# A's scores and softmax split and placed among Newton's steps, q and k loads planned nine steps earlier, W' chunks spread over the batch

## The chip, the cores and the metric

The kernel runs on one core of a Trainium2 chip. The metric is the device time of one execution in microseconds. The core has a matmul engine (TensorE; PE in the profile, with its weight loads as PEld), VectorE (DVE), ScalarE (ACT), GpSimd (POOL), and SyncE (SP), whose queue here issues all data transfers. Each engine works off its own instructions in a fixed order; an instruction that waits holds up everything behind it on that engine.

## What is computed

Three blocks in a row: attention over 32 landmarks for 8 batches of 8 heads, an MLP with an ELU, and a maxout MLP.

```python
q_lm = q.reshape(B, H, m, S // m, D).mean(axis=3)      # B=8, H=8, S=576, D=64, m=32
k_lm = k.reshape(B, H, m, S // m, D).mean(axis=3)
A, Bm, C = sm(q, k_lm), sm(q_lm, k_lm), sm(q_lm, k)    # softmax of scaled scores
Z = Bm.T / (norm1(Bm) * norminf(Bm) + 1e-06)
for _ in range(6):
    Z = 2 * Z - Z @ Bm @ Z
x = heads_to_columns(A @ Z @ C @ v)                    # 4608 x 512
h = x @ w_in                                           # 512 -> 2048
g = where(h > 0, h, exp(min(h, 0)) - 1)
x = g @ w_out                                          # 2048 -> 512
out = maximum(x @ w1, x @ w2, x @ w3) @ w_out2
```

## The kernel before

Fp32 is reached with three matmuls of split operands (high times high, low times high, high times low). The first phase covers attention and the first MLP, the second the maxout MLP; the change touches the first.

**Steps.** The main loop at the end of the kernel function runs 256 steps, 32 for each batch (`NSL`): two halves of 288 tokens times 16 blocks of 128 hidden columns. A step t issues `h_mm` (6 matmuls into `ph`, read from the softmax rows `ah`, `al` and the folded weights W', tile `wp`), then whatever the list `plan[t]` holds, then `h_post` (the end of the ELU on VectorE, tile `eh`, and its split into `gt`), then `x_mm` of step t-3 (12 matmuls into four accumulators `x`). ScalarE does two activations of `eh` and a cast per step. `ph` has two buffers: the `h_mm` of a step needs the `h_post` of the step two earlier.

**Attention.** While batch b-1 goes through its 32 steps, `att_steps(b)` computes what batch b needs: the sums over 18 tokens of q and k (`sums`), C's scores and exponentials (`score_c`), their transposes (`exp_t`), C times v (`cv`), the 32x32 softmax and its norms (`soft_b` to `norm_b`), `bbt`, six Newton steps (`newton`, n0 to n5), A's scores (`score_a`, two halves of 288 tokens, each read from the q tile and transposed on VectorE), A's softmax for two groups of heads (`soft_a1` subtracts the maximum and exponentiates, `soft_a2` sums, `soft_a3` scales, transposes into `af` and splits into `ah` and `al`), and `m_step`, which ends the Newton chain. Then `w_step(b, n)` makes W' chunk n of four: 16 matmuls into the two `banks`, two ScalarE casts, two VectorE subtractions. Chunk n serves hidden blocks 4n to 4n+3; the first `h_mm` of batch b needs chunk 0. All these matmuls pass through the same two PSUM `banks` (in the first stage other ones).

**Loads.** `load_qk` brings a batch's q and k for one group of heads (576 KB each) into tiles of two buffers per tag: one batch's two groups fill both, so the loads of batch b+1 reuse the tiles that A's scores of batch b still read. `Narrowing` converts the second phase's weights twice in each of batches 1 to 6 (batches count from 0): a load of 1 MB into the tile that also holds v (one buffer, free once `cv` of the batch has read v), a burst of four ScalarE activations (L114, L117), two VectorE shifts (L123), two GpSimd additions (L127), a store.

**Order.** The tables `STEP_SLOTS` (batches 2 to 7) and `SECOND_SLOTS` (batch 1) give each attention step the number of a main-loop step; but the final order on every engine is set by the framework's scheduler, which places each instruction by its own estimate of when its operands are there, with the program's order as priority. What then stands where is read from the finished program.

Of the kernel before, what the change touches and what calls it, by code (L numbers as in the profile page):

```python
# [19 lines left out]
def landmark_attention_mlp_maxout_kernel(  # L20
# [336 lines left out]
    def score_a(b):  # L357
        xs_ = [
            att.tile([P, 2 * NB2, M], F32, tag="s", name="x", bufs=3) for _ in range(2)
        ]  # L360
        for half in range(2):
            pas = att_pair(b, "pa")
            heads(
                pas,
                HF,
                lambda j: state["ks", b, j // 2][:, j % 2],
                lambda j: state["q", b, j // 2][:, j % 2, half * HF : (half + 1) * HF],
            )
# [702 lines left out]
    def att_steps(b):  # L1071
# [20 lines left out]
        first += [("a", lambda: score_a(b)), ("m", lambda: m_step(b))]  # L1092
# [17 lines left out]
    def load_att(b):  # L1110
# [72 lines left out]
    for _ in range(NF):  # L1183
# [208 lines left out]
```

## Time and profile before

| | us |
|---|---|
| median of 3 runs (1420.45 to 1422.23) | 1421.42 |
| the profiled execution, its own time | 1420.76 |
| span of its trace, first to last instruction | 1418.6 |
| TensorE busy in the span | 1322.1 (93%) |
| VectorE, GpSimd, ScalarE busy | 868.7, 692.6, 686.6 |

TensorE is the busiest engine. The first phase takes up to some 850 us of the span, in which a batch's 32 steps take 99 to 100 us once all is running. The profile shows for each wait who ended it, and, in slices, the clock that TensorE was granted as a share of full speed (1.00 is 2.4 GHz, 0.50 is 1.2 GHz).

### The profile page before, as it was taken

The numbers are of one execution on the slowest core, as the hardware profiler recorded it, in microseconds if no ns is written. First come the engines' busy times: TensorE is split into PE (matmuls) and PEld (weight loads), VectorE is DVE, ScalarE is ACT, GpSimd is POOL, SyncE is SP. The second block draws the span as 40 slices with busy tenths as digits, with TensorE's granted clock in tenths as the row PEclk, the third lists the DMA queues.
The fourth block names the chain that finished last, engine by engine and source line by source line (L and its number), as shares of the span: only waits on it lengthen the run. The fifth ranks groups of instructions, "written<-read, shape, count | busy, mean of one in ns | idle before, by whom it ended". The sixth has DMA issues, their size and how long they took to land.

```text
span 1418.6 us, 28407 instructions
## 1 busy us (share of the span) xinstructions
PE 1322.1 (93%) x11144; PEld 1236.2 (87%) x11144; DVE 868.7 (61%) x1597; ACT 686.6 (48%) x1554; POOL 692.6 (49%) x677
## 2 busy tenths in 40 slices
PE   2498999899899999898999899899999999999998
PEld 1288899699699698797897899899999999998998
DVE  5866643643644635536445757866776677687773
ACT  4676566455565655664665573322222222335551
POOL 2783334234333333342343566665666666675543
PEclk8589999899999999999999999999999999999999
DMA  9623304203214023033032113212221222148972
GB/s 367 219 73 101 101 18 140 85 26 115 84 41 159 25 88 120 18 113 112 1 107 77 45 33 105 96 53 108 82 83 74 87 83 109 75 141 299 302 253 76
DMA packets 91591, 152.31 MB, mean 107 GB/s; under 512 B 5312, under 2 KB 49472, under 8 KB 91456
## 3 DMA queue, kind: packets, MB, share of 16 engines
q1 hardware_dynamic: 91456, 150.49, 31.0%
q8 instruction: 87, 1.43, 0.4%
q14 instruction: 48, 0.39, 0.1%
HBM read 99.35 MB, written 51.12 MB: 106 GB/s over the span
## 4 chain that ended last, share of the span: by engine, by line
PE 72%; DVE 11%; DMA 5%; issue 4%; ACT 4%; POOL 3%; SPq 0%; DVEq 0%; POOLq 0%; ACTq 0%
PE x L660 23%; PE p L935 23%; PE ph L629 13%; PE p L1044 8%; PE banks L226 5%; POOL u L816 1%; DMA words<-in_moe_w_in_dram 1%; DVE wp L606 1%; DMA hf<-hs 1%; DVE tt L744 1%; DMA qT<-in_q_dram 1%; DMA words<-in_moe_w_dram 1%; DMA kT<-in_k_dram 1%; ACT words L117 1%; DVE af L403 1%
## 5 line engine op out<-in xcount | busy, mean ns | idle before, releaser
L660 PE MATMUL x<-gt,wo 128*128 128x288 f32 x3072 | 467.7, 299 | 4.2 <-ACT xo L686 2.9
L660 PEld LDWEIGHTS x<-gt,wo 128*128 128x128 f32 x3072 | 427.8, 190 | 17.4 <-issue 9.2
L935 PE MATMUL p<-xo,w 128*128 128x256 f32 x3402 | 412.6, 284 | 4.7 <-ACT xo L777 1.7
L935 PEld LDWEIGHTS p<-xo,w 128*128 128x128 f32 x3402 | 410.2, 191 | 7.1 <-ACT xo L777 3.3
L98 POOL TENSOR_TENSOR gt<-eh,gt 128x288 fp32r<-128x288 f32 x243 | 199.6, 825 | 369.2 <-ACT gt L96 339.9
L629 PE MATMUL ph<-ah,wp 128*128 128x288 f32 x1024 | 262.1, 311 | 22.6 <-ACT ah L96 9.8
L629 PEld LDWEIGHTS ph<-ah,wp 128*128 128x128 f32 x1024 | 183.8, 195 | 63.7 <-DVE eh L639 22.1
L639 DVE SCALAR_TENSOR_TENSOR eh<-eh,ph 128x288 f32<-128x288 f32 x256 | 114.9, 452 | 194.0 <-ACT eh L634 173.5
L816 POOL TENSOR_TENSOR u<-s,v 128x512 f32<-128x512 f32 x99 | 137.2, 1386 | 138.1 <-DVE v L814 138.1
L96 ACT CAST gt<-eh 128x288 fp32r<-128x288 f32 x256 | 110.3, 432 | 105.8 <-DVE eh L639 105.6
L629 PE MATMUL ph<-al,wp 128*128 128x288 f32 x512 | 156.1, 306 | 2.6 <-POOL al L98 2.5
L633 ACT ACTIVATE eh<-ph 128x288 f32<-128x288 f32 x256 | 103.8, 410 | 107.7 <-PE ph L629 95.5
L805 ACT COPY s<-p 128x512 f32<-128x512 f32 x99 | 58.0, 586 | 182.5 <-PE p L935 152.1
L1044 PE MATMUL p<-wo,ho 128*128 128x256 f32 x1134 | 136.6, 283 | 5.1 <-ACT ho L1032 3.8
L1044 PEld LDWEIGHTS p<-wo,ho 128*128 128x128 f32 x1134 | 136.0, 190 | 5.7 <-ACT ho L1032 4.2
L634 ACT ACTIVATE eh<-eh 128x288 f32<-128x288 f32 x256 | 112.7, 445 | 5.8
L629 PEld LDWEIGHTS ph<-al,wp 128*128 128x128 f32 x512 | 99.7, 195 | 6.1 <-POOL al L98 5.6
L829 DVE TENSOR_TENSOR t<-p,u 128x512 f32<-128x512 f32 x81 | 55.7, 687 | 65.9 <-POOL u L816 63.0
L942 DVE TENSOR_TENSOR t<-t 128x1024 f32<-128x1024 f32 x54 | 71.5, 1324 | 8.8 <-POOL t L819 3.2
L1034 DVE TENSOR_TENSOR ho<-hf,ho 128x768 fp32r<-128x768 f32 x54 | 66.3, 1254 | 16.3 <-ACT ho L1032 15.8
L127 POOL TENSOR_TENSOR wf<-wf,words 128x512 uint32<-128x512 uint32 x40 | 53.2, 1333 | 40.5 <-ACT words L117 28.8
L1032 ACT CAST ho<-hf 128x768 fp32r<-128x768 f32 x63 | 51.6, 837 | 43.2 <-PE p L1044 23.6
(162 smaller groups left out, 1438.2 us busy)
## 6 DMA issues: line engine op xcount, KB each, us to landing
hf<-hs SPq DMA_DIRECT2D x63, 384.0 KB, 5.2
hs<-t SPq DMA_DIRECT2D x27, 512.0 KB, 2.6
xs<-xo SPq DMA_DIRECT2D x36, 288.0 KB, 2.9
hs<-s SPq DMA_DIRECT2D x27, 384.0 KB, 2.9
qT<-in_q_dram SPq DMA_DIRECT2D x16, 576.0 KB, 5.8
kT<-in_k_dram SPq DMA_DIRECT2D x16, 576.0 KB, 7.0
words<-in_moe_w_dram SPq DMA_DIRECT2D x9, 1024.0 KB, 6.2
xf<-xs SPq DMA_DIRECT2D x9, 1024.0 KB, 5.0
```

The lines of the kernel that those rows point to most:

```text
L96: nc.scalar.copy(hi, src)
L98: eng.tensor_tensor(out=lo, in0=src, in1=hi.bitcast(F32), op=ALU.subtract)
L226: ins = fn(*args, **kw)
L629: nc.tensor.matmul(ph[:, :HF], a, c, start=(g == 0 and j == 0), stop=(g == 1 and j == 2))
L633: nc.scalar.activation(e, ph[:, :HF], AF.Relu, scale=-1.0)
L634: nc.scalar.activation(e, e, AF.Exp, scale=-1.0)
L639: nc.vector.scalar_tensor_tensor(out=e, in0=e, scalar=1.0, in1=ph[:, :HF], op0=ALU.subtract, op1=ALU.max)
L660: nc.tensor.matmul(xacc[ec][:, :HF], a, gt[:, c], start=(first and j == 0), stop=(last and j == 2),)
L816: nc.gpsimd.tensor_tensor(out=u57, in0=s57, in1=v.unsqueeze(1).to_broadcast([P, 2, 256]), op=ALU.add)
L935: nc.tensor.matmul(dst, l, r, start=(c == 0 and j == 0), stop=(c == 1 and j == 2))
L942: nc.vector.tensor_tensor(out=t, in0=t, in1=cur, op=ALU.max)
L1044: nc.tensor.matmul(dst, l, r, start=(c == 0 and n == 0), stop=(c == NP - 1 and n == 2))
```

## The change

`score_a` becomes two steps, `ah0` and `ah1`, one per half of the tokens, planned at steps 10 and 12 (before: one step at 18), between Newton's steps 9 to 14 (before 12 to 17). The softmax pieces of the two groups alternate and each group has its own small tile `t18`. `sums` of batch b move to the last steps of the batch ahead (-6 to -3, before 0 to 3) and the loads of q and k to -9; v stays at 0. The four W' chunks of the next batch are planned at steps 21, 25, 29 and 33, two after the last reader of their place (before 26, 28, 30 and 32). Nothing is computed otherwise; the number of matmuls, transfers and bytes is the same.

```diff
-    def score_a(b):
-        xs_ = [
-            att.tile([P, 2 * NB2, M], F32, tag="s", name="x", bufs=3) for _ in range(2)
-        ]
-        for half in range(2):
-            pas = att_pair(b, "pa")
-            heads(
...
+    def score_a(b, half):
+        if not half:
             for g in range(2):
...
+        pas = att_pair(b, "pa")
+        heads(
...
         for g in range(2):
-            state["x", b, g] = xs_[g]
+            x = state["x", b, g][:, half * NB2 : (half + 1) * NB2]
+            nc.vector.transpose(out=x.rearrange("p a m -> p (a m)"), in_=pas[g][:, :HF])
...
-        t = att.tile([P, 2 * NB2], F32, tag="t18", name="t18")
+        t = att.tile([P, 2 * NB2], F32, tag=f"t18{g}", name="t18")
...
-        first += [("a", lambda: score_a(b)), ("m", lambda: m_step(b))]
+        first += [("ah0", lambda: score_a(b, 0)), ("ah1", lambda: score_a(b, 1)), ("m", lambda: m_step(b))]
...
     STEP_SLOTS = dict(
...
-        bbt=11, n0=12, n1=13, n2=14, n3=15, n4=16, n5=17, a=18, m=19, a10=19, a20=20, a30=20,
-        a11=21, a21=22, a31=23,
+        bbt=8, n0=9, n1=10, n2=11, n3=12, n4=13, n5=14, ah0=10, ah1=12, m=15, a10=12, a11=13,
+        a20=14, a21=15, a30=17, a31=18,
...
+    W_SLOTS = [-11, -7, -3, 1]
 
     def load_att(b):
         for g in range(2):
             load_qk(b, g, "q")
             load_qk(b, g, "k")
-        load_v(b)
...
         if b > 1:
-            at(t0, load_att, b)
+            at(t0 - 9, load_att, b)
+            at(t0, load_v, b)
...
         for n in range(NCH):
-            at(t0 + NSL + 2 * n - 6, w_step, b, n)
+            at(t0 + NSL + W_SLOTS[n], w_step, b, n)
```

What the scheduler makes of it, at four places. Rows give line, operation, output<-inputs and shape; most code lines stand three lower in the changed program (`h_mm` L629 becomes L626, `x_mm` L660 becomes L657).

**The end of the batch ahead of batch 4, TensorE.** `rr` and `rd` are a Newton step's operands, `bbd` is read by `m_step`, `w_in_sb` by a W' chunk. Before, from `m_step` on:

```order
L226 MATMUL banks<-bbd,rr_94 64x128 x2
L629 MATMUL ph<-ah,wp 128x288
L660 MATMUL x_5084<-gt,wo 128x288 x3
L660 MATMUL x_5085<-gt,wo 128x288 x3
L660 MATMUL x_5086<-gt,wo 128x288 x3
L660 MATMUL x_5087<-gt,wo 128x288 x3
L660 MATMUL x_5084<-gt,wo 128x288 x3
L660 MATMUL x_5085<-gt,wo 128x288 x3
L660 MATMUL x_5086<-gt,wo 128x288 x3
L226 MATMUL banks<-w_in_sb,mt 32x512 x8
L660 MATMUL x_5087<-gt,wo 128x288 x3
```

After, around `m_step` and chunk 0:

```order
L657 MATMUL x_5116<-gt,wo 128x288
L657 MATMUL x_5117<-gt,wo 128x288
L226 MATMUL banks<-bbd,rr_94 64x128 x2
L226 MATMUL banks<-w_in_sb,mt 32x512 x8
L626 MATMUL ph<-ah,wp 128x288
L626 MATMUL ph<-al,wp 128x288
L626 MATMUL ph<-ah,wp 128x288
```

and around chunks 1 and 2, four h matmuls further on:

```order
L626 MATMUL ph<-ah,wp 128x288 x2
L626 MATMUL ph<-al,wp 128x288
L226 MATMUL banks<-w_in_sb,mt 32x512 x8
L626 MATMUL ph<-ah,wp 128x288 x2
L226 MATMUL banks<-w_in_sb,mt 32x512 x8
L626 MATMUL ph<-ah,wp 128x288
L626 MATMUL ph<-al,wp 128x288
```

Before, 21 x matmuls stand between `m_step` and chunk 0, 27 more behind it, and only then the new batch's `h_mm`. After, the last Newton step stands 12 x matmuls ahead of the old batch's end, `m_step` behind the last of these, chunk 0 behind `m_step`, the new batch's `h_mm` behind chunk 0; and two h matmuls stand between chunks 1 and 2 (before: six).

**The same place, VectorE.** From the transposes of A's second half on (`t_...` are A's maxima and sums, L270 the q and k sums of the next batch). Before:

```order
L370 STREAM_TRANSPOSE x<-banks 128x288 x2
L381 TENSOR_REDUCE t_5076<-x 128x18
L383 TENSOR_TENSOR x<-x,t_5076 128x576
L270 TENSOR_REDUCE qs<-qT 128x64
L639 SCALAR_TENSOR_TENSOR eh<-eh,ph 128x288
L390 TENSOR_REDUCE t_5110<-x 128x18
L270 TENSOR_REDUCE kT<-kT 128x2x32
```

After, up to the addition of the last but one Newton step:

```order
L378 TENSOR_REDUCE t_4897<-x 128x18
L380 TENSOR_TENSOR x<-x,t_4859 128x576
L636 SCALAR_TENSOR_TENSOR eh<-eh,ph 128x288
L270 TENSOR_REDUCE qs<-qT 128x64
L380 TENSOR_TENSOR x<-x,t_4897 128x576
L270 TENSOR_REDUCE kT<-kT 128x2x32
L513 TENSOR_TENSOR rd<-banks,hm 128x256
L387 TENSOR_REDUCE t_4930<-x 128x18
L636 SCALAR_TENSOR_TENSOR eh<-eh,ph 128x288
L270 TENSOR_REDUCE qs<-qT 128x64
L387 TENSOR_REDUCE t_4964<-x 128x18
L270 TENSOR_REDUCE kT<-kT 128x2x32
```

The four sums still stand between the pieces of A's softmax; two Newton operations (this `rd` and, some rows further on, the additions L566) have come among them, and the W' subtractions (L606, now L603), four of which stood before the second `af`, have gone behind it.

**Batch 0, VectorE.** Around main-loop steps 20 to 25, while batch 1's attention runs. Before:

```order
L639 SCALAR_TENSOR_TENSOR eh<-eh,ph 128x288
L370 STREAM_TRANSPOSE x<-banks 128x288 x2
L381 TENSOR_REDUCE t_1491<-x 128x18
L639 SCALAR_TENSOR_TENSOR eh<-eh,ph 128x288
L270 TENSOR_REDUCE qs<-qT 128x64
```

After:

```order
L372 STREAM_TRANSPOSE x<-banks 128x288 x2
L603 TENSOR_TENSOR wp<-banks,wp 128x512 x2
L372 STREAM_TRANSPOSE x<-banks 128x288 x2
L378 TENSOR_REDUCE t_1390<-x 128x18
L270 TENSOR_REDUCE qs<-qT 128x64
L378 TENSOR_REDUCE t_1431<-x 128x18
L636 SCALAR_TENSOR_TENSOR eh<-eh,ph 128x288 x2
L513 TENSOR_TENSOR rd<-banks,hm 128x256
```

A's scores have moved four steps ahead there, on both sides of a W' chunk of batch 0, and the first q sum of batch 2 has come ahead of two `eh`.

**The middle of a batch, ScalarE.** The second conversion burst, before:

```order
L96 CAST gt<-eh 128x288
L114 ACTIVATE wf_5272<-words_5185 128x512
L117 ACTIVATE words_5185<-words_5185 128x512
L114 ACTIVATE wf_5275<-words_5185 128x512
L117 ACTIVATE words_5185<-words_5185 128x512
L633 ACTIVATE eh<-ph 128x288
```

and after:

```order
L630 ACTIVATE eh<-ph 128x288
L564 COPY rr_94<-banks 128x2x32
L114 ACTIVATE wf_5314<-words_5209 128x512
L117 ACTIVATE words_5209<-words_5209 128x512
L114 ACTIVATE wf_5317<-words_5209 128x512
L631 ACTIVATE eh<-eh 128x288
L117 ACTIVATE words_5209<-words_5209 128x512
```

The burst now stands three steps behind the batch's first burst (before four) and between the two activations of one step's `eh`. The first burst stands behind the two ScalarE copies of `x` into `xo` in the middle of the batch (before: ahead of them).

## Rows read from the trace of the kernel before

**Rows 1.** The page, its first line.
```profile
span 1418.6 us, 28407 instructions
```
**Rows 2.** TensorE by stretches: start:end, length, busy us, granted clock, DMA share, GB/s.
```profile
378.80:458.40 79.60, 79.53 (x710) 1.00 0.23 77
260.00:282.00 22.00, 17.79 (x131) 0.77 0.20 72
...
460.00:482.00 22.00, 18.68 (x149) 0.84 0.16 59
...
660.00:682.00 22.00, 16.98 (x140) 0.92 0.18 66
760.00:782.00 22.00, 20.14 (x177) 1.00 0.42 124
```
**Rows 3.** Chain that ended last: start, us, what; a Newton step, an h step, an x step.
```profile
445.66 0.44 PE banks L226 x4
...
446.24 0.79 PE ph L629 x6
...
450.12 1.62 PE x L660 x12
```
**Rows 4.** TensorE in time at the batch's end: start, us, instruction [idle before].
```profile
453.52 0.71 PE L226 MATMUL banks<-qT,kT 64*32 64x288 f32 x16
...
466.67 1.09 PE L226 MATMUL banks<-w_in_sb,mt 64*32 64x512 f32 x16 [0.28 <-DVE wp L606]
...
470.58 1.73 PE L226 MATMUL banks<-w_in_sb,mt 64*32 64x512 f32 x16 [1.09 <-DVE wp L606]
473.81 0.85 PE L629 MATMUL ph<-ah,wp 128*128 128x288 f32 x2 [1.51 <-ACT ah L96]
```
**Rows 5.** VectorE in time there: the second `af`.
```profile
472.52 0.78 DVE L403 STREAM_TRANSPOSE af<-x 128x576 f32<-128x576 f32 x1
```
**Rows 6.** VectorE groups from 454.3 to 473.4: count, busy us, mean ns, idle before.
```profile
L270 DVE TENSOR_REDUCE qs<-qT 128x64 f32<-128x1152 f32 x2 | 2.7, 1350 | 1.4 <-DMA qT<-in_q_dram 1.4
...
L606 DVE TENSOR_TENSOR wp<-banks,wp 128x512 fp32r<-128x512 f32 x4 | 2.6, 680 | 0.0
```
**Rows 7.** VectorE groups of the whole span: a Newton step's `rd`.
```profile
L516 DVE TENSOR_TENSOR rd<-banks,hm 128x256 f32<-128x256 f32 x35 | 14.7, 420 | 9.9 <-PE banks L226 9.6
```
**Rows 8.** Waits of the SP queue: line, waited for, us, times, longest.
```profile
SPq L252 <- PE banks L226: 83.0, 5, 16.9
```
**Rows 9.** ScalarE groups from 454.3 to 473.4: the casts of W' and `ah`.
```profile
L601 ACT CAST wp<-banks 128x512 fp32r<-128x512 f32 x5 | 2.7, 586 | 2.4 <-PE banks L226 2.3
...
L96 ACT CAST ah<-af 128x288 fp32r<-128x288 f32 x3 | 1.2, 429 | 1.3 <-DVE af L403 1.3
```
**Rows 10.** TensorE in time at batch 0's steps 20 to 26.
```profile
141.94 0.71 PE L226 MATMUL banks<-rr,rd 128*128 128x128 f32 x4 [1.10 <-DVE rr L569]
...
149.72 0.72 PE L226 MATMUL banks<-qT,kT 64*32 64x288 f32 x16
```
**Rows 11.** VectorE in time there: the first q sum.
```profile
154.63 1.35 DVE L270 TENSOR_REDUCE qs<-qT 128x64 f32<-128x1152 f32 x1 [2.22 <-DMA qT<-in_q_dram]
```
**Rows 12.** TensorE in time in the middle of batches 1 and 4.
```profile
214.27 0.90 PE L226 MATMUL banks<-v,et 128*32 128x64 f32 x40
...
512.81 0.90 PE L226 MATMUL banks<-v,et 128*32 128x64 f32 x40
...
524.40 0.67 PE L660 MATMUL x<-gt,wo 128*128 128x288 f32 x3 [1.45 <-ACT xo L686]
```
**Rows 13.** ScalarE in time there: first activations of the conversion bursts.
```profile
220.24 0.69 ACT L114 ACTIVATE wf<-words 128x512 f32<-128x512 f32 x1 [0.17 <-DMA words<-in_moe_w_dram]
...
520.44 0.67 ACT L114 ACTIVATE wf<-words 128x512 f32<-128x512 f32 x1 [2.59 <-DMA words<-in_moe_w_dram]
...
531.49 0.67 ACT L114 ACTIVATE wf<-words 128x512 f32<-128x512 f32 x1 [2.19 <-DMA words<-in_moe_w_dram]
```
**Rows 14.** VectorE in time: the `eh` behind the second burst of batch 4.
```profile
534.73 0.46 DVE L639 SCALAR_TENSOR_TENSOR eh<-eh,ph 128x288 f32<-128x288 f32 x1 [0.24 <-ACT eh L634]
```

More of the change, by code (lines that the diff above doesn't have):

```diff
@@ L355, in score_c2 @@
         state["rs", b, g] = rs
-    def score_a(b):
-        xs_ = [
-            att.tile([P, 2 * NB2, M], F32, tag="s", name="x", bufs=3) for _ in range(2)
-        ]
-        for half in range(2):
-            pas = att_pair(b, "pa")
-            heads(
[L364 to L368, printed above, removed]
+    def score_a(b, half):
+        if not half:
             for g in range(2):
-                nc.vector.transpose(
-                    out=xs_[g][:, half * NB2 : (half + 1) * NB2].rearrange("p a m -> p (a m)"),
-                    in_=pas[g][:, :HF],
-                )
+                state["x", b, g] = att.tile(
+                    [P, 2 * NB2, M], F32, tag="s", name="x", bufs=3
+                )
+        pas = att_pair(b, "pa")
+        heads(
+            pas,
+            HF,
+            lambda j: state["ks", b, j // 2][:, j % 2],
+            lambda j: state["q", b, j // 2][:, j % 2, half * HF : (half + 1) * HF],
+        )
         for g in range(2):
-            state["x", b, g] = xs_[g]
+            x = state["x", b, g][:, half * NB2 : (half + 1) * NB2]
+            nc.vector.transpose(out=x.rearrange("p a m -> p (a m)"), in_=pas[g][:, :HF])
     def soft_a1(b, g):
@@ L388, in soft_a2 @@
     def soft_a2(b, g):
-        t = att.tile([P, 2 * NB2], F32, tag="t18", name="t18")
+        t = att.tile([P, 2 * NB2], F32, tag=f"t18{g}", name="t18")
         nc.vector.tensor_reduce(out=t, in_=state["x", b, g], op=ALU.add, axis=AX.X)
@@ L1099, in landmark_attention_mlp_maxout_kernel @@
     STEP_SLOTS = dict(
-        q0=0, k0=1, q1=2, k1=3, c=5, c20=6, c21=6, e0=6, cv0=7, e1=8, b=8, b2=9, cv1=10, nb=10,
-        bbt=11, n0=12, n1=13, n2=14, n3=15, n4=16, n5=17, a=18, m=19, a10=19, a20=20, a30=20,
-        a11=21, a21=22, a31=23,
+        q0=-6, k0=-5, q1=-4, k1=-3, c=2, c20=3, c21=3, e0=3, cv0=4, e1=5, b=5, b2=6, cv1=7, nb=7,
+        bbt=8, n0=9, n1=10, n2=11, n3=12, n4=13, n5=14, ah0=10, ah1=12, m=15, a10=12, a11=13,
+        a20=14, a21=15, a30=17, a31=18,
     )
@@ L1105, in landmark_attention_mlp_maxout_kernel @@
         q0=4, k0=5, q1=6, k1=7, c=8, c20=9, c21=9, e0=9, cv0=11, e1=11, b=12, b2=12, cv1=13, nb=13,
-        bbt=13, n0=13, n1=14, n2=15, n3=16, n4=18, n5=19, a=20, m=20, a10=21, a20=23, a30=24,
-        a11=26, a21=26, a31=26,
+        bbt=13, n0=13, n1=14, n2=15, n3=16, n4=18, n5=19, ah0=16, ah1=17, m=20, a10=18, a11=19,
+        a20=20, a21=21, a30=22, a31=23,
     )
+    W_SLOTS = [-11, -7, -3, 1]
     def load_att(b):
@@ L1199, in landmark_attention_mlp_maxout_kernel @@
         "V": [lambda g=g, fn=fn: fn(0, g) for g in range(2) for fn in (score_c2, exp_t, cv)],
-        "A": [lambda: score_a(0)]
+        "A": [lambda: [score_a(0, half) for half in range(2)]]
         + [
@@ L1228, in landmark_attention_mlp_maxout_kernel @@
     load_att(1)
+    load_v(1)
     def after_gate(stp):
```

## The prediction

> **What bounds the kernel now.** I read the page first, then TensorE by stretches, then its idle times in order, then what the engines ahead of it did there. The span is 1418.6 us [rows 1]. In the 80 us between two batch ends TensorE is busy 79.53 of 79.60 us at full clock [rows 2]: there only fewer matmuls would help, and the change removes none. An h step costs 0.79 us and an x step 1.62 [rows 3]. What can be won is at the batch ends. In 22 us around each, TensorE is idle 4.2 us ahead of batch 2, 3.3 ahead of batch 4, 5.0 ahead of batch 6, 1.9 ahead of batch 7 (length less busy time) [rows 2]; batches 3 and 5 lie between 4 and 6. I call these ends 2 to 7, by the batch that follows. The granted clock of these stretches, 0.77, 0.84, 0.92 and 1.00, means 10.1, 7.0, 3.5 and 0 us at 1.2 GHz [rows 2].
>
> Why it idles: the second half of A's scores ends near 454.2 [rows 4], and VectorE works without a pause from there until the second `af` at 473.3 [rows 5], except 1.4 us in which the first q sum waits for its load [rows 6]. Two q sums (2.7 us), two k sums like them, four W' subtractions (2.6) and both groups' softmax stand in that one queue [rows 6]; `h_mm` waits for the `ah` at its end (1.51 us), and chunks 1 and 2 for the subtractions of the chunks ahead (0.28 and 1.09) [rows 4]. The plan of the change would break up this queue. What the order shows decides whether it does.
>
> **The loads.** The plan has them nine steps early, but the tile is the one that A's scores of the batch ahead read. SP already waits for TensorE at L252 in 5 batches, 83.0 us in all [rows 8], and the load goes out when A's second half has been read. That half is no earlier in the new order: five and a third x steps ahead of the batch's end before, five and two thirds after, because Newton's chain starts later and is stretched. So q lands some 4 us behind A's end (the first q sum began at 154.63, where A's second half had started at 149.72 and taken 0.72 [rows 10, 11]), and the sums stay where they were in the queue.
> The Trainium skill, DMA: Bandwidth & Descriptors, section Rules for kernel authors, says to issue a transfer early and wait for it late; its section Anatomy of one DMA says that a semaphore wait happens on the issuing sequencer before the transfer is dispatched. The 83.0 us of [rows 8] agree with the second and speak against the first helping here. By the first rule no q sum would wait, and the sum below would be some 4 us smaller, an estimate.
>
> **Ends 3 to 6.** Take A's end as 0. VectorE's list up to the second `af` is the old one (19.1 us, 454.2 to 473.3) without the four W' subtractions (-2.6) [rows 6], with one `eh` (0.46 [rows 14]), one `rd` (0.42) and two additions on half as many columns (0.6 taken) more [rows 7]; and the q sum stands some 1 us further back, so that its wait shrinks from 1.4 to about 0.4. That is 17.0. ScalarE then casts the second group's `ah` twice (0.43 each, the second partly beside the first) and only then chunk 0's high part (0.59) [rows 9], since chunk 0 is now made at the very end: `h_mm` can start near 18.5. TensorE's work up to there is 3 h steps (2.4), 5.67 x steps (9.2), two Newton steps (0.44 each [rows 3]), `m_step` (no more than one of these) and chunk 0 (1.09 [rows 4]), 14.0. So 4.5 us idle, spread over Newton's last step, which waits for an addition queued behind the sums, `m_step`, chunk 0 and `h_mm`. Then chunk 2: before, 2.8 us passed from chunk 1's end (467.76) to chunk 2 (470.58) for two casts and two subtractions [rows 4], with six h matmuls between. After, two (0.27): 2.5 us idle. Together 7.0 against 4.2 (the middle of [rows 2]): +2.8 for each of four ends, +11. The clock I take as before; the idle pieces are longer, so the upper bound has +3 each for it, and the lower bound 0 for the whole place, were VectorE's list 3 us shorter than its rows say.
>
> **End 2.** A's second half stands two x steps earlier, so the chain to chunk 0 finds cover. Two `eh` behind the sums hold up `h_mm` for some 1.9 us and chunk 2 for 2.5: 4.4, against 4.2. But this end has had 10.1 us at the lower clock, the others about 5 [rows 2]; half of the difference is -2. Bounds -5 and +1.
>
> **End 7.** No sums here. Chunk 0 directly ahead of `h_mm` costs its cast and a latency (0.9), chunk 2 again 2.5: 3.4, against 1.9. +2, bounds 0 and +4.
>
> **Batch 0.** The largest single piece. A's scores move ahead to where batch 0 makes its own last W' chunk with nothing else left for TensorE: the two transposes between cost 0.9. Behind A's second half VectorE meets the first q sum at once. Before, that sum began 4.2 us behind A's end (154.63, A ends near 150.4) [rows 10, 11], of which VectorE idled 2.2, and the last `eh` had gone through ahead of it. Now two `eh` stand behind it: 4.2 + 1.35 + 0.7 (a maximum) + 0.4 = 6.6 us until TensorE's next `h_mm` may start, with 0.7 us of work: 5.9 idle. The next two `eh` stand behind three more sums, two reductions, `rd` and an addition, near 13.5, when TensorE has run out near 11.9: 1.6. Less the 1.10 that a Newton step waited there [rows 10]: 0.9 + 5.9 + 1.6 - 1.1 = 7.3, and 2 more for the lower clock behind so long a gap. +9, bounds +4 and +12.
>
> **The middle of batches 1 to 6.** The first conversion burst starts when its load lands behind `cv`: 5.1 us behind it in batch 1 (220.24 against 215.1), 6.7 in batch 4 (520.44 against 513.7) [rows 12, 13]; four batches are like the first, two like the second. In those two the burst held up the copies of `x` for 1.45 us [rows 12]; the copies now stand ahead of it: -2.9 in all. The second burst starts 11.05 us behind the first (531.49 less 520.44) [rows 13], as its load needs the tile back, and the `eh` behind it ends 3.7 us later (535.19) [rows 13, 14]. Counted from `cv`, that is 5.1 or 6.7 + 14.75 = 19.9 or 21.5. By the new order TensorE needs that `eh` after 6 h steps (4.7), 7.33 x steps (11.9), `bbt` and two Newton steps (1.3 [rows 3]) and A's first half (0.7 [rows 4]): 18.6. Stall 1.3 or 2.9; before none, since the burst stood a step later. 4 x 1.3 + 2 x 2.9 = 11; I take +8, since the count of matmuls leaves out the latencies between them, which give the `eh` a little more time. Bounds +1 and +12.
>
> **The sum.** 11 - 2 + 2 + 9 - 2.9 + 8 = +25. Against the profiled execution's own 1420.76 that is 1446; the median of the runs lies 0.7 above it, so 1446.5, rounded to 1446. Phase two is the same work and starts later by the same amount; I count nothing there.
>
> **Rivals.** *The change does what it says.* The plan's places are kept, the queue is broken up, and all idle at the ends goes (five ends at 4.2 and one at 1.9: 23 us) with half of the time at the lower clock that they cost (some 13): 1385. The order speaks against it: `m_step`, planned at step 15 of a batch, stands behind the last x matmul in batches 3 to 6. Chance 0.04. *VectorE's queue no longer decides.* If A's softmax overlaps so much with TensorE that the second `af` comes within 12.5 us of A's end, `h_mm` finds it ready after TensorE's 14.0 us of work: the four ends then lose 2.5 us (chunk 2) instead of 4.2 and about 1 less to the clock, -11 in all; with batch 0 at +4, end 2 at -5 and the middle at -3 + 1: 1407. For it: four subtractions have left the queue. Against it: the rest is still 17 us. 0.13. *It evens out.* The ends equal the old ones, and batch 0's +5 cancels end 2 and the copies: 1418 to 1424. 0.08. *The clock makes it worse.* The longer gaps at the four ends and in batch 0 keep TensorE at 1.2 GHz for some 6 us more each, in which it does half the work: +3 each, 1461. It decides once a gap is followed by as much slow clock as at end 2 (10.1 us [rows 2]). 0.14.
> The Trainium skill, TensorE: Matmul & The Clock Gate, section HAM oscillation, says that a matmul engine that falls idle again and again is throttled again behind each gap, and that this is paid every time. The clock of [rows 2] agrees: it falls at five of the six ends.
>
> **How the numbers follow.** The forecast has 0.61. Its own range takes the bounds that are not all at one end: four ends 0 to +20, end 2 -5 to +1, end 7 0 to +4, batch 0 +4 to +12, middle -2 to +9; about half of each side's spread at once gives 1430 to 1460. To leave out no more than 2 in 10, the range reaches down over the case that evens out and the upper half of the one in which VectorE no longer decides, and up past the clock's 1461: 1411 to 1463. Outside lie the first rival, the lower half of the second (together 0.11) and some 0.08 above. About 0.2% (2.8 us) is what a measurement of this kernel can tell from no change. Faster 0.17, same 0.08, slower 0.75.
>
> **What would show it.** In the changed profile: SP waiting for TensorE at L252 as before; the first q sum of each batch some 4 us behind A's end, in batch 0 with TensorE idle near 6 us for `eh` behind it; at ends 3 to 6 TensorE waiting for Newton's addition, then between `m_step`, chunk 0 and `h_mm`, then over 2 us ahead of chunk 2, 6 to 8 us in all; no wait for `xo` in mid-batch, but 1 to 3 us for `eh` behind the second burst. Wrong would be: loads that go out before A's end; an end with under 4 us idle; or TensorE held back nowhere between the ends.

## The result: 1.1% slower, 15 us, and the profile after

The changed kernel takes 1437.06 us (median of 4 runs, 1435.96 to 1440.76) against 1421.83; the ratio is 1.0112 with a 95% interval of 1.0088 to 1.0136. The forecast of 1446 had the sign and lies 9 us too high. The profiled execution is the longest of the four (1440.76), 20.0 us above that of before, so differences between the two traces run some 5 us above those of the medians.

The first line of the page of after [rows 1]:

```profile
span 1439.0 us, 28404 instructions
```

TensorE of after in 22 us around ends 2, 4, 6 and 7 and around batch 0's place (columns as in [rows 2]):

```profile
260.00:282.00 22.00, 19.01 (x159) 15.14 (x158) 12.25 (x25) 12.51 (x32) 8.95 (x11) 0.96 0.08 28
...
467.00:489.00 22.00, 15.56 (x116) 9.64 (x115) 14.45 (x26) 9.73 (x25) 6.23 (x8) 0.84 0.16 60
...
672.00:694.00 22.00, 15.52 (x119) 10.26 (x118) 14.76 (x27) 9.64 (x25) 6.09 (x8) 0.91 0.16 60
777.00:799.00 22.00, 18.74 (x168) 14.04 (x167) 10.45 (x21) 12.64 (x32) 7.37 (x9) 1.00 0.43 124
136.00:158.00 22.00, 14.30 (x114) 11.59 (x115) 14.17 (x28) 7.41 (x18) 4.64 (x5) 0.84 0.29 108
```

Length less busy time: end 4 is idle 6.4 us (before 3.3 [rows 2]), end 6 6.5 (5.0), end 7 3.3 (1.9), end 2 3.0 (4.2, and the clock went from 0.77 to 0.96; a wait of 0.7 us stands just ahead of this window). TensorE at end 4, in time (start, us, instruction, idle before and what ended it):

```profile
460.08 0.71 PE L226 MATMUL banks<-qT,kT 64*32 64x288 f32 x16
...
473.64 0.71 PE L226 MATMUL banks<-rr,rd 128*128 128x128 f32 x4 [1.44 <-DVE rr L566]
...
476.26 0.44 PE L226 MATMUL banks<-bbd,rr 128*64 128x128 f32 x4 [0.33 <-DVE rr L566]
477.07 1.09 PE L226 MATMUL banks<-w_in_sb,mt 64*32 64x512 f32 x16 [0.36 <-ACT mt L586]
479.62 0.40 PE L626 MATMUL ph<-ah,wp 128*128 128x288 f32 x1 [1.46 <-ACT wp L598]
...
486.33 1.96 PE L226 MATMUL banks<-w_in_sb,mt 64*32 64x512 f32 x16 [1.78 <-DVE wp L603]
```

Newton's last step waits for an addition, `m_step` for the next, chunk 0 for M's copy, `h_mm` for chunk 0's cast, chunk 2 for chunk 1's subtractions: the chain that was forecast, in that order. VectorE there: the first q sum, the last k sum with the Newton addition behind it, the second `af`:

```profile
464.71 1.35 DVE L270 TENSOR_REDUCE qs<-qT 128x64 f32<-128x1152 f32 x1 [0.61 <-DMA qT<-in_q_dram]
...
471.68 1.34 DVE L270 TENSOR_REDUCE kT<-kT 128x64 f32<-128x1152 f32 x1
472.94 0.44 DVE L636 SCALAR_TENSOR_TENSOR eh<-eh,ph 128x288 f32<-128x288 f32 x1
473.30 0.28 DVE L566 TENSOR_TENSOR rr<-banks,rr 128x128 f32<-128x128 f32 x1
...
477.53 0.75 DVE L400 STREAM_TRANSPOSE af<-x 128x576 f32<-128x576 f32 x1
```

The first q sum stands 3.9 us behind A's end (460.79), and SP still waits for TensorE before it may load (waits of the SP queue):

```profile
SPq L252 <- PE banks L226: 48.5, 5, 10.2
```

In batch 0, TensorE waits 4.85 us for an `eh` that stands behind the first q sum, itself 4.2 us behind A's end (142.57). At end 2 it waits twice for an `eh` that stands behind the sums; and in batch 3 an `eh` comes late behind the second conversion burst. No wait for `xo` over 0.3 us is left between batches 1 and 6. TensorE of after, in time:

```profile
149.17 0.61 PE L626 MATMUL ph<-ah,wp 128*128 128x288 f32 x1 [4.85 <-DVE eh L636]
...
258.47 0.40 PE L626 MATMUL ph<-ah,wp 128*128 128x288 f32 x1 [0.71 <-DVE eh L636]
...
262.01 0.40 PE L626 MATMUL ph<-ah,wp 128*128 128x288 f32 x1 [0.89 <-DVE eh L636]
...
448.08 0.40 PE L626 MATMUL ph<-ah,wp 128*128 128x288 f32 x1 [1.68 <-DVE eh L636]
```

VectorE of after in batch 0, the q sum and the two `eh` behind it:

```profile
146.74 1.35 DVE L270 TENSOR_REDUCE qs<-qT 128x64 f32<-128x1152 f32 x1 [2.55 <-DMA qT<-in_q_dram]
...
148.67 0.81 DVE L636 SCALAR_TENSOR_TENSOR eh<-eh,ph 128x288 f32<-128x288 f32 x2
```

**The loop.** The prediction did not use one view, which carries most of what follows: when C's first scores (`banks<-kT,qs`) and `m_step` (`banks<-bbd`) of each batch run. TensorE of before, in time: chunk 3, C's scores, M, and C's scores of the next batch:

```profile
377.55 1.64 PE L226 MATMUL banks<-w_in_sb,mt 64*32 64x512 f32 x16
...
383.29 0.72 PE L226 MATMUL banks<-kT,qs 64*32 64x288 f32 x16
...
457.98 0.44 PE L226 MATMUL banks<-bbd,rr 128*64 128x128 f32 x4
...
481.98 0.71 PE L226 MATMUL banks<-kT,qs 64*32 64x288 f32 x16
```

The same of after (its M is the row at 476.26 above):

```profile
389.46 1.09 PE L226 MATMUL banks<-w_in_sb,mt 64*32 64x512 f32 x16
...
395.99 0.72 PE L226 MATMUL banks<-kT,qs 64*32 64x288 f32 x16
...
500.65 0.72 PE L226 MATMUL banks<-kT,qs 64*32 64x288 f32 x16
```

Both kernels run W' chunk 3 ahead of C's scores: both use the two `banks`, each use is issued behind the one before it, and chunk 3 is planned first. Chunk 3 needs M, M needs Newton, Newton needs C's scores of its batch. That is a closed loop, one turn per batch. In this batch M comes 74.7 us behind C's scores before and 80.3 after (476.26 less 395.99), and the next batch's C's scores 24.0 and 24.4 behind M. So in the changed kernel the loss lies between C's scores and M, where A now stands between Newton's steps. The table in the next section has these figures for every run.

### The profile page after: what moved, and what is told of

Same layout as the page of the kernel before. It is cut to its first block, busy times and chain, and to the rows that moved or that the text cites. A ratio compares the mean times of both kernels' runs of the same rounds, so it can differ in the third digit from the quotient of the medians.

```text
span 1439.0 us, 28404 instructions
## 1 busy us (share of the span) xinstructions
PE 1328.3 (92%) x11144; PEld 1241.3 (86%) x11144; DVE 863.6 (60%) x1597; ACT 684.3 (48%) x1554; POOL 691.3 (48%) x677
## 4 chain that ended last, share of the span: by engine, by line
PE 70%; DVE 7%; DMA 4%; POOL 4%; issue 3%; ACT 2%; SPq 0%; DVEq 0%; POOLq 0%; ACTq 0%
PE p L932 22%; PE x L657 21%; PE ph L626 13%; PE p L1041 8%; PE banks L226 5%; POOL u L813 1%; DMA words<-in_moe_w_dram 1%; DMA qT<-in_q_dram 1%; DVE wp L603 1%; DMA hf<-hs 1%; ACT wp L598 1%; POOL t L816 1%; DVE tt L741 1%; DVE kT L270 1%; DVE qs L270 1%
## 5 line engine op out<-in xcount | busy, mean ns | idle before, releaser
L657 PE MATMUL x<-gt,wo 128*128 128x288 f32 x3072 | 464.0, 300 | 3.0 <-ACT gt L96 2.5
L657 PEld LDWEIGHTS x<-gt,wo 128*128 128x128 f32 x3072 | 427.6, 190 | 10.0 <-ACT gt L96 4.5
L626 PE MATMUL ph<-ah,wp 128*128 128x288 f32 x1024 | 264.3, 317 | 30.2 <-DVE eh L636 17.2
L626 PEld LDWEIGHTS ph<-ah,wp 128*128 128x128 f32 x1024 | 185.8, 199 | 80.3 <-issue 31.6
L626 PE MATMUL ph<-al,wp 128*128 128x288 f32 x512 | 156.8, 307 | 0.0
L626 PEld LDWEIGHTS ph<-al,wp 128*128 128x128 f32 x512 | 101.8, 199 | 0.5 <-issue 0.5
L603 DVE TENSOR_TENSOR wp<-banks,wp 128x512 fp32r<-128x512 f32 x64 | 41.2, 686 | 74.5 <-ACT wp L598 74.4
L1031 DVE TENSOR_TENSOR ho<-hf,ho 128x768 fp32r<-128x768 f32 x54 | 64.9, 1227 | 17.5 <-ACT ho L1029 17.0
```

The costliest lines, as they stand in the source:

```text
L626: nc.tensor.matmul(ph[:, :HF], a, c, start=(g == 0 and j == 0), stop=(g == 1 and j == 2))
L657: nc.tensor.matmul(xacc[ec][:, :HF], a, gt[:, c], start=(first and j == 0), stop=(last and j == 2),)
```

## The experiments

"Turn" is the time from C's scores of batch 2 to those of batch 7 over five; C to M and M to C are means over six and five batches of the profiled execution; "idle" is TensorE's from 200 to 700 us, length less busy time. "Clock lost" is the full-clock time that was not granted, (1 - mean granted clock) times span, a mean over all executions of a run. Ratios are to the kernel before, measured beside each run, with 95% intervals.

| run | median us | ratio | turn | C to M | M to C | idle | clock lost |
|---|---|---|---|---|---|---|---|
| before | 1421.83 | 1 | 99.7 | 75.0 | 24.6 | 24.0 | 48 to 49 |
| changed | 1437.06 | 1.0112 (1.0088 to 1.0136) | 103.9 | 78.8 | 24.5 | 31.0 | 53.9 |
| e1_second_back | 1434.47 | 1.0098 (1.0079 to 1.0118) | 103.0 | 78.5 | 23.9 | 29.4 | 48.7 |
| e2_a_behind_newton | 1448.42 | 1.0199 (1.0179 to 1.0220) | 104.5 | 75.5 | 29.0 | 38.4 | 65.8 |
| e3_loads_w_back | 1434.18 | 1.0106 (1.0085 to 1.0127) | 102.7 | 78.7 | 23.2 | 30.7 | 49.9 |
| e4_c_ahead_of_chunk3 | 1418.52 | 0.9980 (0.9965 to 0.9996) | 98.9 | 78.9 | 20.1 | 22.0 | 49.6 |
| e5_one_t18 | 1433.29 | 1.0084 (1.0061 to 1.0108) | 100.9 | 74.9 | 26.3 | 24.8 | 59.2 |
| e6_short_sums | 1431.83 | 1.0062 (1.0038 to 1.0086) | 102.5 | 77.1 | 25.1 | 25.0 | 54.2 |
| e7_c_early_w2_w3 | 1428.78 | 1.0048 (1.0030 to 1.0066) | 100.3 | 85.6 | 14.4 | 26.5 | 55.6 |
| e8_w2_w3_in_c | 1424.24 | 1.0011 (0.9997 to 1.0026) | 100.1 | 83.9 | 16.2 | 21.0 | 53.4 |
| e9_split_one_t18 | 1434.74 | 1.0086 (1.0065 to 1.0106) | 101.9 | 76.9 | 24.9 | 27.1 | 55.2 |
| e10_c_early_two_t18 | 1411.83 | 0.9931 (0.9907 to 0.9955) | 97.4 | 78.7 | 18.5 | 17.3 | 38.9 |
| e11_z1_two_t18 | 1419.92 | 0.9984 (0.9966 to 1.0002) | 101.0 | 83.1 | 17.3 | 22.4 | 42.9 |
| e12_changed_c_ahead | 1414.44 | 0.9941 (0.9924 to 0.9958) | 98.1 | 80.6 | 17.4 | 16.5 | 42.8 |

The last column bounds how much of a difference can be clock (a bound, since part of it falls into idle time): of the changed list's 12 to 15 us (its own run and e3, the same list) 2 to 5, of e1's 12 under 1, of e9's 13 some 6, of e5's 11 some 10; e10's gain of 10 comes with 10 us less of it. What sets the clock in each run is not shown.

### Which part of the change costs

**Loads, sums and W' slots set back.**

```diff
-        q0=-6, k0=-5, q1=-4, k1=-3, c=2, ...
+        q0=0, k0=0, q1=1, k1=1, c=2, ...
-    W_SLOTS = [-11, -7, -3, 1]
+    W_SLOTS = [-6, -4, -2, 0]
-            at(t0 - 9, load_att, b)
+            at(t0, load_att, b)
```

> The changed kernel with the q and k loads, their sums and the W' chunks set back to the slots of the kernel before (loads at the batch's start, sums at steps 0 and 1, chunks at -6, -4, -2 and 0); A stays between Newton's steps. Theory (these parts do nothing, since the loads wait for A's second half in any case and the chunks for M): 1434 to 1440, each end within 1 us of the changed kernel's. Rival (the sums ahead of the activations, or chunks that stand too close, carry the loss): 5 us or more faster, 1432 or less.

1434.18, as the theory had it; more than that, the lists of all five engines came out the same, row for row, as those of the changed kernel. Three parts of the change (loads, sums, W' slots) change nothing in this program, since operands and tiles come free no earlier; W' chunk 3 is planned ahead of C's scores in both. So this run is a second measurement of the changed kernel: 2.9 us between the medians is how well one is known.

**Batch 1's table set back.**

```diff
     SECOND_SLOTS = dict(
-        ..., ah0=16, ah1=17, m=20, a10=18, a11=19, a20=20, a21=21, a30=22, a31=23,
+        ..., ah0=20, ah1=20, m=20, a10=21, a20=23, a30=24, a11=26, a21=26, a31=26,
```

> The changed kernel with one table set back: A's scores and softmax of batch 1, computed in batch 0, stand again where the kernel before has them; all else as changed. Theory (places add up): the place in batch 0 is a loss of its own, some 8 us by the shift between the two traces (0.1 us at h step 16 of batch 0, 8.0 at step 16 of batch 1). Expected 1429, TensorE idle in batch 0's steps 20 to 26 about 3.4 us as before, full clock there. Rival (the loops even out): what batch 0 loses is only lent, since the attention of batch 1 then starts the next loop later or earlier; the time changes by less than 3 us and the loss appears at end 2 instead.

1434.47, against 1437.06 and 1434.18 for the changed list: 0 to 2.6 us faster where the theory had 8, as the rival has it. The way that the rival names is not shown. At step 16 of batch 1 (by the count of `h_mm`) e1 stands at 218.4, the changed kernel at 223.7 and e3 at 225.9; at step 16 of batch 5 they stand at 625.7, 629.5 and 625.7. So e1 keeps 3.8 of 5.3 us against one trace of the changed list, and nothing of 7.5 against the other. Between these two points, TensorE of e1, of e3 and of the changed kernel (columns as in [rows 2]):

```profile
218.41:625.72 407.31, 383.87 (x3301) 343.87 (x3300) 198.41 (x471) 223.60 (x555) 139.74 (x164) 0.96 0.23 79
225.93:625.73 399.80, 375.46 (x3259) 338.39 (x3258) 198.07 (x467) 224.18 (x556) 139.92 (x164) 0.98 0.23 77
223.74:629.50 405.76, 381.25 (x3258) 341.86 (x3257) 198.27 (x467) 224.26 (x556) 139.94 (x164) 0.96 0.23 76
```

All three are idle for 23.4 to 24.5 us there, so e1 does not wait longer at the ends; against e3 it runs at a lower clock. Where the rest of batch 0's loss goes stays open.

**A set back behind Newton.**

```diff
-        ..., ah0=10, ah1=12, m=15, a10=12, a11=13, a20=14, a21=15, a30=17, a31=18,
+        ..., ah0=15, ah1=15, m=15, a10=15, a11=16, a20=16, a21=17, a30=17, a31=18,
```

> The changed kernel with A's two halves and their softmax of batches 2 to 7 set back behind Newton's last step (slots 15 to 18); batch 1's table, the loads, the sums and the W' slots stay as changed. Theory (A between Newton's steps): with A's halves and softmax between, the chain from the first score of C to the product M takes 80.3 us in the changed kernel (396.0 to 476.3) and 74.7 before (383.3 to 458.0); that is what makes M and the first W' chunk meet a TensorE that has nothing left. Expected: idle at ends 3 to 6 back from 6 to 7 us to some 4.3 each, no Newton step that waits over 1 us, time 1423 to 1428. Rival (the tables of loads, sums and W' do it): the ends keep their 6 us, 1434 to 1440.

Neither: 1448. C to M fell to 75.5, as the theory asked, but M to C rose to 29.0. TensorE of e2 at end 4, chunks 0 and 1:

```profile
474.15 1.09 PE L226 MATMUL banks<-w_in_sb,mt 64*32 64x512 f32 x16
482.25 1.96 PE L226 MATMUL banks<-w_in_sb,mt 64*32 64x512 f32 x16 [7.02 <-DVE wp L603]
```

VectorE of e2 ahead of it, the last k sum and the first subtraction:

```profile
479.58 1.34 DVE L270 TENSOR_REDUCE kT<-kT 128x64 f32<-128x1152 f32 x1
480.84 0.68 DVE L603 TENSOR_TENSOR wp<-banks,wp 128x512 fp32r<-128x512 f32 x1
```

Chunk 1 waits 7 us: chunk 0's subtractions stand behind both groups' softmax and all four sums. With a tile each, the groups run interleaved; with one tile the second group had waited for the first, and the subtractions had gone between. The next run undoes just that, on top of e2:

```diff
-        t = att.tile([P, 2 * NB2], F32, tag=f"t18{g}", name="t18")
+        t = att.tile([P, 2 * NB2], F32, tag="t18", name="t18")
```

> The kernel of e2_a_behind_newton (changed kernel, A of batches 2 to 7 behind Newton) with one edit more: the two softmax groups of A share one small tile again (t18 instead of t180 and t181), as in the kernel before. Theory (the two tiles cost e2 its ends): with two tiles both groups' softmax run interleaved on VectorE, so that chunk 0's subtractions wait behind both and behind four sums (in e2 they ran at 480.84, 5.6 us behind their matmul, before 3.8 us with the sums ahead) and both `ah` are ready only at the end; TensorE stood 7 to 8.5 us ahead of chunk 1. With one tile the second group waits for the first. Expected: C's scores 99 to 101 us apart as before, 1419 to 1427 (batch 0 keeps the changed table, which cost nothing in the end). Rival (the early slots of Newton, sums or W' do it): 1440 or more, with 7 us ahead of chunk 1.

15 us faster than e2: there the second tile is the cost (from the end of chunk 0's matmuls to its first subtraction it is 5.6 us in e2 and 2.8 before), and the turn is back near the old one (100.9). The time is not: 1433, outside both expectations. In lists of all engines this kernel differs from the kernel before with only batch 1's new table by a few swapped rows. These are not free: at the ends from 2 to 6 VectorE now takes the second group's maximum ahead of the first group's `af`, and `h_mm` waits for the first `ah`, which it did not before. VectorE of e5 at end 4:

```profile
473.55 0.74 DVE L378 TENSOR_REDUCE t<-x 128x18 f32<-128x576 f32 x1
474.21 0.77 DVE L400 STREAM_TRANSPOSE af<-x 128x576 f32<-128x576 f32 x1
```

VectorE of before there:

```profile
466.53 0.77 DVE L403 STREAM_TRANSPOSE af<-x 128x576 f32<-128x576 f32 x1
467.22 0.71 DVE L381 TENSOR_REDUCE t<-x 128x18 f32<-128x576 f32 x1
```

TensorE of e5:

```profile
475.50 0.53 PE L626 MATMUL ph<-ah,wp 128*128 128x288 f32 x2 [0.71 <-ACT ah L96]
```

So the 11 us of e5 are not the price of batch 1's table alone. At step 16 of batch 2 e5 is 5.4 us behind the kernel before (321.5 against 316.1; C's scores of batch 2 stand at 188.19 against 183.81). The other 6 come at the later ends, which have the swapped rows: up to step 16 of batch 7, 1.3 us more idle time and 7 us more of full clock lost. Beside the slower loop the table costs 0 to 2.6 us (e1); what it costs without that loop is at most 11 us, and no run shows it by itself.

**A between Newton's steps alone.** The lists of e1 are row for row those of the kernel before with nothing but A moved and two tiles. With one tile:

```diff
-        ..., n5=17, a=18, m=19, a10=19, a20=20, a30=20, a11=21, a21=22, a31=23,
+        ..., n5=17, ah0=13, ah1=15, m=18, a10=15, a11=16, a20=17, a21=18, a30=20, a31=21,
```

> The kernel before with one part of the change alone: A's two halves of batches 2 to 7 stand between Newton's steps, their softmax beside them, but with the one small tile t18 of the kernel before; batch 1's table, loads, sums and W' as before. (e1_second_back came out as the same part with two tiles: +1.0%.) Theory (A's second half stands no earlier against the batch's end, and Newton's last two steps, M and the first W' chunk now come behind it): the loss belongs to A's new place, with one tile as with two, 1432 to 1438; C's first scores to M near 79 us. Rival (the second tile is what costs here too, as it did in e2 against e5, 15 us): 1421 to 1426.

1434.74: A's new place costs 12 to 13 us, with one tile as with two (1.0086 and 1.0098, intervals overlapping); C to M is 76.9, less than the 79 expected. So most of the loss comes with A's place. Batch 1's table costs 0 to 2.6 us beside it (at most 11 without it), the second tile costs 15 us with A behind Newton (e2 and e5) and nothing here, and loads, sums and W' slots do nothing as long as A stands between Newton's steps.

### What sets the loss at the ends

**The sums cut to a quarter.**

```diff
-            in_=t[:, :, :S].rearrange("p r (m j) -> p r m j", j=GS),
+        n = GS if b < 2 else 4
+            in_=t[:, :, : M * n].rearrange("p r (m j) -> p r m j", j=n),
```

> The changed kernel with the q and k sums of batches 2 to 7 over 4 of each 18 columns (part of the computation left out): each about 0.4 us of VectorE instead of 1.35, four per batch, so some 3.8 us less in VectorE's queue at each batch's end. Theory (my prediction's: VectorE's queue at the ends, sums included, holds up Newton's last additions and what follows): idle at ends 3 to 6 falls from 6 or 7 us by 3 to 4 each, turn of C's scores from 103.4 to some 100, 1413 to 1424. Rival (latencies between the engines set the chain from C's scores to M, VectorE has room): less than 5 us faster, 1431 or more.

Nearer the rival: 1431.83, 2 to 5 us less than the changed list by the medians and 6 or 7 by the ratios, where the theory had 13 or more, for 3.8 us less of VectorE at each end with sums. TensorE of e6 at end 4:

```profile
471.66 0.44 PE L226 MATMUL banks<-bbd,rr 128*64 128x128 f32 x4 [0.60 <-DVE rr L567]
473.71 1.09 PE L226 MATMUL banks<-w_in_sb,mt 64*32 64x512 f32 x16 [1.61 <-ACT mt L587]
...
482.52 1.87 PE L226 MATMUL banks<-w_in_sb,mt 64*32 64x512 f32 x16 [2.12 <-DVE wp L604]
```

Newton's last step no longer waits 1.44 us, but chunk 0 now waits 1.61 for M's copy, and chunk 2 2.12. The queue that I had summed is there, but a shorter one hands over to the chain of single waits behind it.

**C's scores ahead of chunk 3, in the kernel before.**

```diff
-            at(t0 + NSL + 2 * n - 6, w_step, b, n)
+            at(t0 + NSL + (-6, -4, -2, 6)[n], w_step, b, n)
```

> The kernel before with one number changed: W' chunk 3 is planned six steps into the batch instead of at its start, so that the first scores of C go to the two score banks ahead of it. Theory (a closed loop sets the period): C's scores wait for chunk 3, chunk 3 for M, M for Newton, Newton for C's scores, and one turn of this loop takes the whole batch (C's scores 98.7 us apart, 383.3 and 482.0, with TensorE's own work 95). C then starts some 2 steps earlier and A's second half ends with 1.9 us more of TensorE's work left: idle at ends 3 to 6 down from 4.2 to some 2.3 us and half of what they cost in clock back, 1405 to 1413. Rival (VectorE's queue behind A's end is all that counts, wherever the loop stands): the ends keep 4 us, 1419 to 1424.

1418.52, just under the rival's range and far from the theory's. M to C is 4.5 us shorter, but chunk 3 now falls into C's chain, and C to M is 3.9 longer. At the end itself, VectorE's queue still holds up chunk 2 (TensorE of e4 at end 4):

```profile
471.57 1.27 PE L226 MATMUL banks<-w_in_sb,mt 64*32 64x512 f32 x16 [3.55 <-DVE wp L606]
```

Two bolder versions move C's scores ahead of chunks 2 and 3 and start sums and loads earlier; they differ in where the two chunks go. The steps of `STEP_SLOTS` not shown move 4 or 5 slots ahead:

```diff
-            at(t0 + NSL + 2 * n - 6, w_step, b, n)
+            at(t0 + NSL + [-6, -4, 1, 2][n], w_step, b, n)    # e7; e8: [-6, -4, 2, 3]
-        q0=0, k0=1, q1=2, k1=3, c=5, ...
+        q0=-5, k0=-4, q1=-3, k1=-2, c=0, ...
```

> The kernel before with its loop opened: q and k loads planned 6 steps ahead of the batch's start (behind A), sums at -5 to -2, C's scores at 0 ahead of W' chunks 2 and 3 (planned at 1 and 2 instead of -2 and 0), and all later steps of the attention 4 to 5 slots earlier; A whole and behind Newton, as before. Theory (the closed loop of attention sets the period: with C's scores some 2 h steps earlier in TensorE's list, A's second half stands 4 h steps and 7.7 x steps ahead of the batch's end instead of 2 and 5.3): idle at ends 3 to 6 down from 4.2 to 1 or 2 us, half of the clock's cost gone, 1398 to 1410. Rival (e4 again: what is won in front is lost to C's chain waiting for chunks 2 and 3): 1415 to 1422.

> As e7_c_early_w2_w3, but W' chunks 2 and 3 planned at 2 and 3, so that they stand together behind the first transposes of C's softmax, six to eight h steps into the batch. Theory (loop): C's chain gets on earlier still than in e7 but meets two chunks in a row, so about the same, 1398 to 1412. Rival (two chunks in a row hold up TensorE for ScalarE's casts and VectorE's subtractions, as ahead of chunk 2 in e4): 3 us per batch lost again, 1415 to 1425.

1428.78 and 1424.24, no gain; e7 is above both its ranges, e8 in its rival's. M to C falls by 10.2 and 8.4 us, and C to M rises by 10.6 and 8.9: what a chunk leaves in front of C's scores, it takes again inside the chain.

**With two tiles.** e4 and e8 with the second `t18`:

```diff
-        t = att.tile([P, 2 * NB2], F32, tag="t18", name="t18")
+        t = att.tile([P, 2 * NB2], F32, tag=f"t18{g}", name="t18")
```

> e4_c_ahead_of_chunk3 (W' chunk 3 behind C's scores) with A's softmax groups in two small tiles, A behind Newton. In e2 two tiles brought the last `ah` 15.8 us behind A's end (469.34 to 485.12) instead of 19.6, but chunk 0's subtractions stood behind four sums and both groups. Theory (interleaved groups push chunk 0's subtractions back whatever else is done): over 5 us ahead of chunk 1 at each end, 1430 or more. Rival (with C further ahead the earlier `ah` counts): 1412 to 1417, faster than e4.

> e8_w2_w3_in_c with two small tiles. A's second half stands 3 h steps and 7 x steps ahead of the batch's end, some 16 us of TensorE's work, against 15.8 us to the last `ah` in e2. Theory (as for e10: chunk 1 waits for chunk 0's subtractions): 1428 or more. Rival (the ends close): 1408 to 1418.

e10 takes 1411.83, 0.7% less than before: my theory was wrong, and the time is just under the rival's range. TensorE of e10 at end 4:

```profile
464.98 0.53 PE L629 MATMUL ph<-ah,wp 128*128 128x288 f32 x2 [0.53 <-ACT ah L96]
...
470.88 1.01 PE L226 MATMUL banks<-kT,qs 64*32 64x288 f32 x16 [1.82 <-DVE wp L606]
```

and in 22 us around it (columns as in [rows 2]):

```profile
459.00:481.00 22.00, 18.57 (x155) 13.93 (x154) 12.96 (x29) 10.87 (x29) 7.07 (x9) 0.92 0.08 28
```

The long waits ahead of chunk 1 (7.02 us in e2) and chunk 2 (3.55 in e4) are gone. The same tile costs 15 us in e2 and saves 7 between e4 and e10. e11 (1419.92) lies between its two expectations, and its interval overlaps that of e8, so no gain is shown there.

**The changed kernel with C's scores ahead of chunk 3.** The last run changes one number of the changed kernel:

```diff
-    W_SLOTS = [-11, -7, -3, 1]
+    W_SLOTS = [-11, -7, -3, 3]
```

> The changed kernel with one number changed: W' chunk 3 planned at step 3 of the batch instead of 1, so that C's first scores stand ahead of it (as in e4 and e10); A stays between Newton's steps, with two tiles. In TensorE's list A's second half then has 4 h steps and 7.2 x steps to the batch's end behind it instead of 3 and 5.7, some 3.2 us more work. Theory (what counts is how much of the old batch is left for TensorE when A's second half is done, and C's place behind chunk 3 sets it): some 3 us per turn less, 1418 to 1426, idle at ends 3 to 6 down from 6 or 7 to some 3 to 4 us. Rival (with A between Newton's steps the last two steps, M and chunk 0 come one behind the other at the end in any case): 1431 or more.

1414.44: 22.6 us less than the changed kernel (19.7 less than e3) and 0.6% less than before, more than the theory had. TensorE of e12, from A's second half at end 4 on:

```profile
445.18 0.72 PE L226 MATMUL banks<-qT,kT 64*32 64x288 f32 x16
...
460.24 0.44 PE L226 MATMUL banks<-bbd,rr 128*64 128x128 f32 x4
460.61 2.39 PE L657 MATMUL x<-gt,wo 128*128 128x288 f32 x16
462.92 1.09 PE L226 MATMUL banks<-w_in_sb,mt 64*32 64x512 f32 x16
464.98 0.40 PE L626 MATMUL ph<-ah,wp 128*128 128x288 f32 x1 [0.97 <-ACT wp L598]
...
470.82 1.09 PE L226 MATMUL banks<-w_in_sb,mt 64*32 64x512 f32 x16 [2.10 <-DVE wp L603]
...
477.55 0.72 PE L226 MATMUL banks<-kT,qs 64*32 64x288 f32 x16
...
489.16 1.09 PE L226 MATMUL banks<-w_in_sb,mt 64*32 64x512 f32 x16
```

VectorE of e12, both `af` of that end:

```profile
461.61 1.58 DVE L400 STREAM_TRANSPOSE af<-x 128x576 f32<-128x576 f32 x2
```

VectorE's queue is as long as it was: the second `af` ends 17.3 us behind A's end (445.90 to 463.19; 17.5 in the changed kernel). What is new is what TensorE still has to do: 16 x matmuls, 2.4 us, stand between `m_step` and chunk 0, where the changed kernel has none. From A's second half to `m_step` it works without a wait over 0.3 us at this end (in the changed kernel 0.66, 1.44 and 0.33). C's scores run 11.6 us ahead of chunk 3; M to C is 7.1 us shorter than in the changed kernel, and C to M only 1.8 longer. The wait ahead of chunk 2 is still there (2.10 us; 1.78 in the changed kernel). Of the 22.6 us up to 11 are clock (42.8 us lost instead of 53.9).

The Trainium skill, Perfetto Trace Analysis, section Matmuls, says that independent groups of matmuls should rotate through different PSUM banks, so that reading one out overlaps the next group. W' chunk 3 and C's scores are independent and share two banks. No run here shows what banks of their own would give: e12 and its 22.6 us change the order in which the two use the banks, not the banks.

## Why the prediction was right, and where its terms were off

The steps in their order, the profile beside the forecast:

- **Loads and sums** stay where they were: right. SP waits at L252, the q sum comes 3.9 us behind A's end (about 4 forecast), and e3 shows that these parts change nothing.
- **Ends 3 to 6**: 6.0 to 6.5 us idle where 7.0 was forecast, so +2.1 each for +2.8, some 8 for 11. The second `af` came at 17.5 us behind A's end at end 4 (477.53 + 0.75 less 460.79; 17.0 forecast), `h_mm` at 18.8 (18.5). Chunk 2 waited 1.8 to 2.1 us instead of 2.5.
- **End 2**: -2 forecast, almost -5 found, the lower bound. The two `eh` behind the sums cost 0.7 and 0.9 us (1.9 forecast) and chunk 2 2.1 (2.5), so 3.7 us idle instead of 4.2; and the clock of its 22 us was 0.96 instead of 0.77, 4.2 us of full clock. By the prediction's own sign, an end with under 4 us idle, this end speaks against it.
- **End 7**: +1.4 for +2.
- **Batch 0**: +9 forecast and found at the place itself: the waits from 135 to 150 us add up to 8.7 us instead of 3.4, of it 4.85 behind the q sum where 5.9 was forecast, and 3.5 us for the clock (0.84 in 22 us). The second wait of 1.6 us did not come. But e1, which undoes this place, gains only 0 to 2.6 us: the term is in the trace and mostly not in the time.
- **The middle**: the copies' -2.9 came. The late `eh` behind the second burst cost 2.3 us in all (0.3, 1.7 and 0.4 in batches 2, 3 and 6) where I took 8 of bounds from 1 to 12. This term was mis-sized: the `eh` ended 18.1 to 20.5 us behind `cv`, not 19.9 or 21.5; in batch 3 TensorE wanted it at 18.9 (18.6 counted).
- **The clock** was taken as before at ends 3 to 6. From step 16 of batch 2 to step 16 of batch 7, 22 us of full clock were lost in this trace, 12 in that of before and 10 in that of e3. So it held in e3 and not here; over all executions the changed list lost 2 to 5 us more.

Without this last item that is 8 - 5 + 1.4 + 9 - 2.9 + 2.3, some 13 us, where 25 was forecast; 15.2 were measured, 12 in e3, and 20 between the two traces. So most of the waits that the steps name were there, and the wrong 12 us lie in the burst, end 2 and the ends. Some of the nearness is luck: the sum holds 9 us that hardly count and leaves out the clock. And the range, 1411 to 1463, holds the old time as well.

As an explanation it holds less well. The step "That half is no earlier in the new order" took A's place against the batch's end as given and summed VectorE's queue behind it. What gives A its place is, at least in part, the loop through chunk 3 and the banks, which I did not look for. e6 shows it from one side (3.8 us taken out of the queue give about 1 us per end), e12 from the other (the queue as long as it was, one number of W' changed, 22.6 us). None of the rivals named that mechanism. A's place between Newton's steps is harmful only where chunk 3 stands ahead of C's scores: with C ahead of it A's new place gives 1414 (e12), where A behind Newton gives 1418 with one tile (e4) and 1412 with two (e10). The loop is not all, though: in the kernel before, the same edit gave 0.2% (e4), and bolder ones nothing (e7, e8).

What stays open: why chunk 3 inside C's chain costs 1.8 us in e12 but 3.9 in e4, why undoing batch 0's place gains so little, and what sets the lost clock, up to 10 us of the differences.

## What to carry to other kernels

Where work for the next round is done beside the current one, look for the closed loop (what does the next round's first step wait for, buffers and their order included) and time its two halves in the trace before summing the waits at the seam: here one number on the edge that closed it was worth more than all parts of the change. Compare the finished instruction lists first: parts of a plan whose operands come no earlier changed nothing, and two swapped rows at each end kept e5 from being a test of one table. Undo parts one at a time and in pairs, since a part (here a second small tile) can cost 15 us in one order and save 7 in another. A loss that a trace shows at its place is not yet a loss of time: undo it and measure. And look at the clock of all executions before a difference of 10 us is put down to waits.

## What the runs showed of the hardware that was not expected

One and the same list of instructions, the changed kernel's and e3's, gave spans of 1439.0 and 1431.7 us in their profiled executions, with a granted clock of 0.96 and 0.98 between 200 and 700 us: half a per cent that no instruction explains. And in these runs the idle time of a stretch alone does not give its clock: in 459 to 481 us TensorE of the kernel before is idle 3.3 us at a clock of 0.84, that of e10 3.4 us at 0.92 (its row stands with e10). The kernel before:

```profile
459.00:481.00 22.00, 18.68 (x147) 12.26 (x146) 18.01 (x31) 11.69 (x27) 6.89 (x8) 0.84 0.21 76
```
